# Cross attention and a max-out layer on one core: layer 1 of the first two batches from S W1 + S (-W2), and the softmax of later batches moved from layer 1 to layer 2

## The chip, the cores and the metric

The kernel runs on one core of one Trainium2 chip. The metric is the time of one execution on the device in microseconds (us), and lower is better. TensorE (PE) multiplies matrices, VectorE (DVE), ScalarE (ACT) and GpSimd (POOL) do elementwise work and reductions, and SyncE (SP) issues nearly all transfers. Each engine takes its instructions from a queue of its own, in the order in which the program names them; the order is written by hand here, and waits between engines follow from the data.

## The reference, cut to what matters

For each of 8 batches and 8 heads, 512 positions x and 32 states S, both 64 wide, read each other by attention. Both results of a batch are put together (512 + 32 rows of 8 x 64 = 512 columns) and go through a max-out layer with one pair of weights (512 x 1024) and an output weight (1024 x 512).

```python
def _attn_ref(x, state):                # x (8, 8, 512, 64), state (8, 8, 32, 64)
    scale = 1.0 / np.sqrt(D)
    a = softmax(scale * x @ state^T)      # 512 x 32 for each batch and head
    xread = a @ state
    a2 = softmax(scale * state @ x^T)     # 32 x 512
    sread = a2 @ x
    return concatenate([xread, sread], axis=2)

def _moe_ref(x, w1, w2, w_out):         # x: 8 * 544 rows of 512
    h1 = x @ w1
    h2 = x @ w2
    g = np.maximum(h1, h2)
    return g @ w_out
```

(The softmaxes are written out in the original, with the maximum subtracted.)

Two identities carry the kernel. First, max(h1, h2) = relu(h1 - h2) + h2, so out = relu(x (W1 - W2)) W_out + x (W2 W_out). Second, xread = a S, so that xread (W1 - W2) = a (S (W1 - W2)) with only 32 states a head: S W is made once for each batch, and layer 1 is A^T against it. The kernel keeps W1 - W2 and W2 W_out side by side in `wcat`, 1024 and 512 columns; "S W" is S times the first part (two pieces of 512 columns), "S Wc" times the second (the third piece).

## The kernel before

The parts that the change touches; cuts are marked with "...". `copy("A" | "V" | "P", ...)` is a copy on ACT, DVE or POOL. `bank()` takes the next of eight PSUM banks, which comes free when what it held eight takings earlier has been read out.

```python
    ...  # load_states(hb), cast_states(hb), states(hb): load, cast and transpose the states of half the batches into the block-diagonal sbd; after the change, of a slice of batches
    def compact_x(b, g):
        if g == 0:
            st[b]["xc"] = at.tile([128, H, NC * D], BF16, tag="xc", name="xc")
        copy("A", st[b]["xc"][:, 4 * g:4 * g + 4], xf_t[b][:, 4 * g:4 * g + 4])


    def d_xt(b):
        nc.sync.dma_start_transpose(out=st[b]["xt"], in_=st[b]["xc"].rearrange("p h w -> p (h w)"))
    ...
    def u_sc(b, g, mul=nc.gpsimd):
        u_exp(b, g)
        u_norm(b, g, mul)

    def u_exp(b, g):
        ...  # tiles
        p = bank()
        for i in range(4):
            for cp in range(2):
                k = 2 * i + cp
                nc.tensor.matmul(p[:, k * 64:k * 64 + 64],
                                 d["xt"][:, 4 * i + 2 * g + cp, :], sbd[:, b, 2 * i + g].rearrange("p u n -> p (u n)"),
                                 start=(k == 0), stop=(k == 7))
        nc.scalar.activation(out=d["e"][:, g].rearrange("p i c n -> p (i c n)"), in_=p, func=ACTF.Exp, scale=scale)

    def u_norm(b, g, mul):
        d = st[b]
        nc.vector.tensor_reduce(d["es"][:, g], d["e"][:, g].rearrange("p i c n -> p (i c) n"),
                                axis=mybir.AxisListType.X, op=ALU.add)
        nc.vector.reciprocal(d["er"][:, g], d["es"][:, g])
        mul.tensor_mul(
            d["a"][:, g].rearrange("p c i n -> p i c n"), d["e"][:, g],
            d["er"][:, g].rearrange("p (i c) -> p i c", i=4).unsqueeze(3).to_broadcast([128, 4, NC, Ns]))

    ...  # u_sr: the state's read, 32 small matmuls; u_at, u_xt: transposes on TensorE
    def d_at(b):
        AT[b] = keep.tile([128, 2, NC * 128], BF16, tag="at", name="aT")
        nc.sync.dma_start_transpose(out=AT[b].rearrange("p g (c t) -> p (g c) t", t=128),
                                    in_=st[b]["a"].rearrange("p g c i n -> p (g c i n)"))
    ...
    def u_sw(b, ch):
        pg = [bank(), bank()]
        for i in range(4):
            for g in range(2):
                nc.tensor.matmul(pg[g][32 * i:32 * i + 32, :], sbd[64 * g:64 * g + 64, b, 2 * i + g, g, :],
                                 wcat[64 * g:64 * g + 64, i, ch * 512:(ch + 1) * 512],
                                 start=True, stop=True)
        for g in range(2):
            copy("A" if g else "V", SW[b][:, g, ch * 512:(ch + 1) * 512], pg[g])
    ...  # u_sw01(q, engs): the same for batches 0 and 1 together, 256 columns: see the diff
    ...  # relu: on ACT or DVE, in turn where no engine is named
    def l1(b, fill, fs=range(NF), engs=None):
        if fs[0] == 0:
            R[b] = big.tile([128, NF, NC * 128], BF16, tag="r", name="r")
        for f in fs:
            p = bank()
            for g in range(2):
                nc.tensor.matmul(p, SW[b][:, g, f * 128:(f + 1) * 128], AT[b][:, g, :], start=(g == 0), stop=(g == 1))
            relu(R[b][:, f, :], p, engs and engs[f - fs[0]])
            run(*fill.get(f, ()))

    def l2(b, fill):
        r = R.pop(b)
        ob = big.tile([128, NC, DM], F32, tag="ob", name="ob")
        dst = out[b * L:b * L + S].rearrange("(p c) n -> p c n", c=NC)
        for c in range(NC):
            p = bank()
            cs = slice(c * 128, (c + 1) * 128)
            for g in range(2):
                nc.tensor.matmul(p, AT[b][:, g, cs], SW[b][:, g, FF:WC], start=(g == 0), stop=False)
            for f in range(NF):
                nc.tensor.matmul(p, r[:, f, cs], wo[:, f, :], start=False, stop=(f == NF - 1))
            copy("A" if c % 2 else "V", ob[:, c, :], p)
            if b == B - 1:
                nc.sync.dma_start(out=dst[:, c:c + 1], in_=ob[:, c:c + 1])
            run(*fill.get(NF + c, ()))
        if b < B - 1:
            nc.sync.dma_start(out=dst, in_=ob)
    ...
    def w_sub(q):
        cs = slice(q * 256, (q + 1) * 256)
        nc.vector.tensor_sub(wcat[:, :, cs], w1f[:, :, cs], w2f[:, :, cs])
    ...  # w_cast: W2 to bfloat16 on POOL; w_t: its transposes; w_wo: W2 W_out and its copy on ACT to wcat; ahead, fillers: see the diff
    for b in range(B):
        SW[b] = swt[:, b % 2]
    warm_up(9)
    cast_states(0)
    states(0)
    cast_x(0, (("V", slice(0, 4, 2)), ("A", slice(4, 8, 2)), ("V", slice(1, 4, 2)), ("P", slice(5, 8, 2))))
    u_xt(0, 0, "V")
    u_xt(0, 1, "A")
    u_sc(0, 0, nc.vector)
    u_sc(0, 1, nc.gpsimd)
    cast_x(1, (("P", slice(0, 4, 2)), ("P", slice(4, 8, 2)), ("A", slice(1, 4, 2)), ("A", slice(5, 8, 2))))
    w_cast(0)
    u_sr(0)
    u_xt(1, 0, "A")
    u_xt(1, 1, "V")
    u_at(0, "V")
    u_exp(1, 0)
    u_exp(1, 1)
    u_norm(1, 0, nc.gpsimd)
    u_norm(1, 1, nc.gpsimd)
    u_srt(0)
    nc.gpsimd.dma_start(out=wo, in_=moe_w_out.rearrange("(k p) n -> p k n", p=128))
    w_sub(0)
    w_sub(1)
    w_cast(1)
    u_sw01(0, "AA")
    u_at(1, "A")
    l1(0, {}, range(0, 2), "AA")
    l1(1, {}, range(0, 2), "VA")
    u_sw01(1, "VA")
    u_sr(1)
    w_t(0, 0, "V")
    l1(0, {}, range(2, 4), "AV")
    l1(1, {}, range(2, 4), "AA")
    w_sub(2)
    w_sub(3)
    u_srt(1)
    w_t(0, 1, "A")
    u_sw01(2, "AA")
    l1(0, {}, range(4, 6), "AA")
    l1(1, {}, range(4, 6), "VA")
    u_sw01(3, "VA")
    w_t(1, 0, "V")
    l1(0, {}, range(6, 8), "AV")
    l1(1, {}, range(6, 8), "AV")
    w_t(1, 1, "A")
    cast_x(2)
    compact_x(2, 0)
    compact_x(2, 1)
    d_xt(2)
    for i in range(4):
        w_wo(i)
    cast_states(1)
    u_sw(0, 2)
    u_sw(1, 2)
    ahead(3)
    l2(0, {8: [lambda: u_sc(2, 0), lambda: d_xt(3)], 9: [lambda: u_sc(2, 1)], 10: [lambda: u_sr(2)], 11: [lambda: d_at(2), lambda: u_srt(2)]})
    ahead(4)
    l2(1, {8: [lambda: u_sc(3, 0), lambda: d_xt(4), lambda: u_sw(2, 0)], 9: [lambda: u_sc(3, 1), lambda: u_sw(2, 1)],
           10: [lambda: u_sr(3), lambda: u_sw(2, 2)], 11: [lambda: d_at(3), lambda: states(1), lambda: u_srt(3)]})
    for b in range(2, B):
        fill = fillers(b)
        if b + LEAD + 1 < B:
            ahead(b + LEAD + 1)
        l1(b, fill)
        l2(b, fill)
        if b == B - 2:
            moe_sread()
```

A "slot" is a place in the loop: slots 0 to 7 follow the eight feature blocks of layer 1 (`l1`), slots 8 to 11 the four chunks of layer 2 (`l2`).

Of the kernel before, what the change touches and what calls it, by code (L numbers as in the profile page):

```python
# [15 lines left out]
def kernel(  # L16
# [46 lines left out]

    def run(*units):
        for u in units:
            u()
# [11 lines left out]
    def load_states(hb):  # L78
        nc.sync.dma_start(out=s_f[:, B * hb:B * hb + B],
                          in_=state[B // 2 * hb:B // 2 * hb + B // 2].rearrange("b (q h) n d -> (h n) (b q) d", q=2))  # L80

    load_states(0)
# [9 lines left out]
    load_states(1)  # L92
# [10 lines left out]
    w2b = stage.tile([128, 4, FF], BF16)  # L103
# [10 lines left out]
    def cast_states(hb):  # L114
        qs = slice(B * hb, B * hb + B)
        copy("V", s_bf[:, qs], s_f[:, qs].unsqueeze(2).to_broadcast([128, B, 2, D]))

    def states(hb):
        p = bank(BF16)
        for q in range(B):  # L120
            nc.tensor.transpose(p[:, q * 128:(q + 1) * 128], s_bf[:, B * hb + q].rearrange("p u d -> p (u d)"), ident)
        for g in range(2):
            copy("V", sbd[64 * g:64 * g + 64, B // 2 * hb:B // 2 * hb + B // 2, :, g, :],
                 p[64 * g:64 * g + 64].rearrange("p (b h n) -> p b h n", b=B // 2, h=H))
# [112 lines left out]
    def u_sw01(q, engs):  # L237
        pg = [bank(), bank()]
        for b in range(2):
            for i in range(4):  # L240
                for g in range(2):
                    nc.tensor.matmul(pg[g][32 * i:32 * i + 32, b * 256:(b + 1) * 256],  # L242
                                     sbd[64 * g:64 * g + 64, b, 2 * i + g, g, :],
                                     wcat[64 * g:64 * g + 64, i, q * 256:(q + 1) * 256],
                                     start=(b == 0), stop=(b == 1))
        for g in range(2):
            copy(engs[g], swt[:, :, g, q * 256:(q + 1) * 256], pg[g].rearrange("p (b w) -> p b w", b=2))
# [23 lines left out]
    def l2(b, fill):  # L271
# [3 lines left out]
        for c in range(NC):  # L275
            p = bank()
            cs = slice(c * 128, (c + 1) * 128)
            for g in range(2):
                nc.tensor.matmul(p, AT[b][:, g, cs], SW[b][:, g, FF:WC], start=(g == 0), stop=False)  # L279
            for f in range(NF):  # L280
                nc.tensor.matmul(p, r[:, f, cs], wo[:, f, :], start=False, stop=(f == NF - 1))  # L281
# [34 lines left out]
    def w_cast(ch):  # L316
        cs = slice(ch * 512, (ch + 1) * 512)
        for i in range(0, 4, 2):
            copy("P", w2b[:, i:i + 2, cs], w2f[:, i:i + 2, cs])

    def w_t(ch, half, eng):
        p = bank(BF16)
        for j in range(2):
            for k in range(4):
                f = 4 * ch + k
                nc.tensor.transpose(p[:, (4 * j + k) * 128:(4 * j + k + 1) * 128],
                                    w2b[:, 2 * half + j, f * 128:(f + 1) * 128], ident)
# [3 lines left out]
    def w_wo(i):  # L331
# [3 lines left out]
        copy("A", wcat[:, i, FF:WC], p)  # L335


    def ahead(n):
        if n < B:
            cast_x(n)  # L340
            compact_x(n, 0)
            compact_x(n, 1)
        if n + 1 < B:
            load_x(n + 1)

    def fillers(b):
        fill = {}
        n = b + LEAD
        if n < B:
            for slot, u in ((4, lambda: u_sc(n, 0)), (6, lambda: u_sc(n, 1)), (8, lambda: u_sr(n)),  # L350
                            (10, lambda: d_at(n)), (11, lambda: u_srt(n))):
                fill.setdefault(slot, []).append(u)
        if n + 1 < B:
            fill.setdefault(8, []).append(lambda: d_xt(n + 1))
        if b + 1 < B:
            for slot, ch in ((3, 0), (7, 1), (9, 2)):
                fill.setdefault(slot, []).append(lambda ch=ch: u_sw(b + 1, ch))
        return fill
# [3 lines left out]
    warm_up(9)  # L362
    cast_states(0)
    states(0)
    cast_x(0, (("V", slice(0, 4, 2)), ("A", slice(4, 8, 2)), ("V", slice(1, 4, 2)), ("P", slice(5, 8, 2))))
    u_xt(0, 0, "V")
    u_xt(0, 1, "A")
    u_sc(0, 0, nc.vector)
    u_sc(0, 1, nc.gpsimd)
    cast_x(1, (("P", slice(0, 4, 2)), ("P", slice(4, 8, 2)), ("A", slice(1, 4, 2)), ("A", slice(5, 8, 2))))  # L370
    w_cast(0)
    u_sr(0)
    u_xt(1, 0, "A")
# [84 lines left out]
```

## Time and profile before

| What | Value |
|---|---|
| Time, median of 3 runs | 171.58 us (169.97 to 173.24) |
| Span of the profiled run | 171.0 us |
| Busy: PE, DVE, ACT, POOL | 147.7, 80.3, 74.6, 36.8 us |
| Layer 2's matmuls r W_out (L281) | 253 recorded, 61.4 us busy, 379 ns each |
| Layer 1's matmuls (L267) | 120 recorded, 33.6 us busy, 409 ns each |
| Subtraction W1 - W2 on DVE (L314) | 4, 1797 ns each |
| Cast xc on ACT for the next batches (L58) | 12, 1054 ns each |
| Relus: ACT (L255), DVE (L257) | 35 of 608 ns, 29 of 673 ns |
| Product a on POOL (L182) | 15, 1113 ns each |
| Transposing transfers xt (6) and aT (6), issue to landing, median | 7.0 and 2.9 us |

How to read it: matmuls overlap, so that a row's busy time is longer than TensorE needs for them; where 8 stand in a row, the time from first to first is what one costs. PEld is the loading of weights into TensorE, beside its matmuls. The groups name lines of the kernel: L58, L60 and L62 are the copies on ACT, DVE and POOL for whatever tile; L154, L195, L213 and L230 are transposes of x, the state's read, the transposes of a and S W; L242 is S W of the first two batches, L172 the scores, L175 the exp, L179 and L181 the sum and its reciprocal, L279 and L281 layer 2, L295 the first layer for the states' rows, L326 the transposes of W2, L334 W2 W_out. Releasers are inferred: "PE <- DVE wcat" says that PE's wait ended when DVE had written wcat.

### The profile page before, as it was taken

To read this page: it belongs to the slowest core of one execution; us is meant where nothing else is said; L and a number is where in the kernel's file an instruction comes from. 1 tells how busy PE (TensorE), PEld (TensorE's weight loads), DVE (VectorE), ACT (ScalarE), POOL (GpSimd) and SP (SyncE) were. 2 spreads that over 40 slices of the span, in tenths; PEclk is the share of its full clock that TensorE was granted. 3 is DMA by queue.
4 is the path that set the end of the run, shared out by engine and by line. 5 is a ranking of instruction groups with operands and counts; after the bars stand their busy time and mean duration, and the time that the engine had idled before them with its cause. 6 is when DMAs were issued, how large, how long until landed. Compare 5 with 4: busy or idle time off the path is not lost.

```text
span 171.0 us, 3071 instructions
## 1 busy us (share of the span) xinstructions
PE 147.7 (86%) x1270; PEld 69.8 (41%) x1289; DVE 80.3 (47%) x139; ACT 74.6 (44%) x131; POOL 36.8 (22%) x44
## 2 busy tenths in 40 slices
PE   6554469499979999997998899799999999999991
PEld 2343434234425444443442344244434444744440
DVE  5561775926033446567345524832763643223410
ACT  3171355757665073690277119422802722305111
POOL 3108397400002604405302510400130000000000
PEclk9965558969999999999999999999999999999999
DMA  5999999800496289999459937620520500324033
GB/s 150 340 390 386 376 312 236 145 2 0 88 266 131 64 235 297 219 274 241 103 171 263 180 65 255 116 61 4 245 51 12 230 19 0 161 88 107 15 123 125
DMA packets 34366, 27.99 MB, mean 164 GB/s; under 512 B 21424, under 2 KB 30640, under 8 KB 33456
## 3 DMA queue, kind: packets, MB, share of 16 engines
q1 hardware_dynamic: 33312, 26.74, 55.1%
q0 software_dynamic: 1040, 1.05, 3.8%
q8 instruction: 10, 0.16, 0.4%
q14 instruction: 4, 0.03, 0.1%
HBM read 15.20 MB, written 8.91 MB: 141 GB/s over the span
## 4 chain that ended last, share of the span: by engine, by line
PE 69%; DVE 13%; ACT 11%; issue 3%; POOL 1%; DVEq 0%; ACTq 0%; POOLq 0%
PE ps L281 29%; PE ps L267 11%; PE ps L279 7%; DVE es L179 5%; PE ps L334 4%; ACT xc L58 3%; DVE r L257 3%; PE ps L230 2%; ACT r L255 2%; PE ps L109 2%; DVE wcat L314 2%; PE ps L295 2%; PE ps L305 2%; ACT e L175 2%; PE ps L154 2%
## 5 line engine op out<-in xcount | busy, mean ns | idle before, releaser
L281 PE MATMUL ps<-wo,r 128*128 128x512 bf16 x253 | 61.4, 379 | 3.7 <-DVE r L257 3.3
L281 PEld LDWEIGHTS <-r 128*128 128x128 bf16 x256 | 24.7, 98 | 35.9 <-DVE r L257 6.8
L267 PE MATMUL ps<-aT,swt 128*128 128x512 bf16 x120 | 33.6, 409 | 1.3 <-ACT swt L58 0.7
L58 ACT COPY ob<-ps 128x512 f32<-128x512 f32 x16 | 9.4, 585 | 57.0 <-PE ps L281 42.8
L182 POOL TENSOR_TENSOR a<-e,er 128x512 bf16<-128x512 bf16 x15 | 16.6, 1113 | 78.0 <-ACT e L175 37.4
L257 DVE TENSOR_SCALAR r<-ps 128x512 bf16<-128x512 f32 x29 | 19.4, 673 | 19.7 <-PE ps L267 19.4
L255 ACT ACTIVATE r<-ps 128x512 bf16<-128x512 f32 x35 | 20.8, 608 | 6.2 <-PE ps L267 4.7
L60 DVE CAST swt<-ps 128x512 bf16<-128x512 f32 x22 | 14.8, 678 | 17.4 <-PE ps L230 16.5
L60 DVE COPY ob<-ps 128x512 f32<-128x512 f32 x16 | 11.0, 688 | 20.2 <-PE ps L281 20.2
L279 PE MATMUL ps<-swt,aT 128*128 128x512 bf16 x57 | 17.7, 381 | 1.2 <-issue 0.6
L58 ACT CAST swt<-ps 128x512 bf16<-128x512 f32 x26 | 15.2, 598 | 7.7 <-PE ps L242 4.3
L267 PEld LDWEIGHTS <-swt 128*128 128x128 bf16 x128 | 11.6, 103 | 15.1 <-issue 3.9
L179 DVE TENSOR_REDUCE es<-e 128x16 f32<-128x512 bf16 x16 | 10.8, 678 | 11.3 <-ACT e L175 11.3
L62 POOL CAST xp<-xf 128x2048 bf16<-128x2048 f32 (+1 forms) x9 | 13.1, 1463 | 10.8 <-DMA xf<-in_x_dram 10.8
L58 ACT CAST xc<-xf 128x1024 bf16<-128x1024 f32 x12 | 12.0, 1054 | 0.0
L175 ACT ACTIVATE e<-ps 128x512 bf16<-128x512 f32 x16 | 9.8, 617 | 1.8 <-PE ps L172 1.8
L230 PE MATMUL ps<-wcat,sbd 64*32 64x512 bf16 x160 | 8.4, 386 | 0.5 <-ACT wcat L58 0.3
L172 PEld LDWEIGHTS <-xt 128*128 128x128 bf16 x128 | 6.2, 104 | 3.8 <-DVE xt L60 0.5
L154 PE MATMUL ps<-ident,xp 128*64 128x128 bf16 x64 | 3.1, 267 | 5.2 <-POOL xp L62 3.2
L172 PE MATMUL ps<-sbd,xt 128*128 128x64 bf16 x128 | 6.8, 202 | 0.9 <-ACT xt L58 0.4
L279 PEld LDWEIGHTS <-aT 128*128 128x128 bf16 x64 | 4.6, 97 | 6.7 <-issue 3.9
L334 PE MATMUL ps<-wo,w2t 128*128 128x512 bf16 x32 | 7.1, 379 | 0.0
(56 smaller groups left out, 101.8 us busy)
## 6 DMA issues: line engine op xcount, KB each, us to landing
xf<-in_x_dram SPq DMA_DIRECT2D x7, 1024.0 KB, 9.2
out_dram<-ob SPq DMA_DIRECT2D x7, 1024.0 KB, 4.4
w2f<-in_moe_w_dram SPq DMA_DIRECT2D x2, 1024.0 KB, 11.9
w1f<-in_moe_w_dram SPq DMA_DIRECT2D x2, 1024.0 KB, 13.4
xf<-in_x_dram SPq DMA_DIRECT2D x2, 512.0 KB, 4.6
wo<-in_moe_w_out_dram POOLq DMA_DIRECT2D x1, 1024.0 KB, 11.8
out_dram<-ob SPq DMA_DIRECT2D x4, 256.0 KB, 2.0
s_f<-in_state_dram SPq DMA_DIRECT2D x2, 256.0 KB, 9.7
```

What stands on the lines that cost most here:

```text
L58: nc.scalar.copy(o, i)
L60: nc.vector.tensor_copy(o, i)
L62: nc.gpsimd.tensor_copy(o, i)
L175: nc.scalar.activation(out=d["e"][:, g].rearrange("p i c n -> p (i c n)"), in_=p, func=ACTF.Exp, scale=scale)
L179: nc.vector.tensor_reduce(d["es"][:, g], d["e"][:, g].rearrange("p i c n -> p (i c) n"), axis=mybir.AxisListType.X, op=ALU.add)
L182: mul.tensor_mul(d["a"][:, g].rearrange("p c i n -> p i c n"), d["e"][:, g], d["er"][:, g].rearrange("p (i c) -> p i c", i=4).unsqueeze(3) ...
L255: nc.scalar.activation(out=o, in_=p, func=ACTF.Relu)
L257: nc.vector.tensor_scalar(o, p, scalar1=0.0, scalar2=None, op0=ALU.max)
L267: nc.tensor.matmul(p, SW[b][:, g, f * 128:(f + 1) * 128], AT[b][:, g, :], start=(g == 0), stop=(g == 1))
L279: nc.tensor.matmul(p, AT[b][:, g, cs], SW[b][:, g, FF:WC], start=(g == 0), stop=False)
L281: nc.tensor.matmul(p, r[:, f, cs], wo[:, f, :], start=False, stop=(f == NF - 1))
L334: nc.tensor.matmul(p, w2t[:, i, f, :], wo[:, f, :], start=(f == 0), stop=(f == NF - 1))
```

## The change

Two parts.

At the head, batches 0 and 1 need S (W1 - W2) before anything of layer 1 can start, and the subtraction of full-precision weights on DVE stands between the weights' landing and S W. The change multiplies S with W1 and with -W2 and lets PSUM add the two: twice the matmuls, and casts of W1 and negations of W2 to bfloat16 in place of the subtraction. The casts are spread over ACT, DVE and POOL. The negated copy also serves for the transposes behind W2 W_out, whose sign is turned back when the product is read out. The subtraction, which the later batches and the states' rows still need, moves behind layer 1 of batches 0 and 1. The states come in two loads with batches 0 and 1 alone in the first, and their block-diagonal copies are made in three steps (2, 3 and 3 batches). The warm-up has 5 matmuls in place of 9, and the order of the first softmaxes is different.

In the steady part, scores, exp, sums and products of batch b + 2, the casts xc of batch b + 3 and S W of batch b + 1 were spread over layer 1 and layer 2 of batch b. They are now all in the four slots of layer 2; layer 1 holds its matmuls and relus. The transposing transfer of xc moves from slot 8 to slot 11, behind that of a. In layer 2 of batch 0, the matmuls with W_out come ahead of those with S Wc.

The diff, cut:

```diff
...
+    def negate(eng, o, i):
+        if eng == "A":
+            nc.scalar.activation(out=o, in_=i, func=ACTF.Copy, scale=-1.0)
+        else:
+            (nc.vector if eng == "V" else nc.gpsimd).tensor_scalar(o, i, scalar1=-1.0, scalar2=None, op0=ALU.mult)
+
     def run(*units):
...
-    def load_states(hb):
-        nc.sync.dma_start(out=s_f[:, B * hb:B * hb + B],
-                          in_=state[B // 2 * hb:B // 2 * hb + B // 2].rearrange("b (q h) n d -> (h n) (b q) d", q=2))
-
-    load_states(0)
+    def load_states(bs):
+        nc.sync.dma_start(out=s_f[:, 2 * bs.start:2 * bs.stop],
+                          in_=state[bs].rearrange("b (q h) n d -> (h n) (b q) d", q=2))
+
+    first, rest = slice(0, 2), (slice(2, 5), slice(5, 8))
+    load_states(first)
     load_x(0, 2)
...
     load_x(2)
-    load_states(1)
+    load_states(slice(2, 8))
     load_x(3)
...
     wcat = consts.tile([128, 4, WC], BF16)
-    w2b = stage.tile([128, 4, FF], BF16)
+    w1b = stage.tile([128, 4, FF], BF16)
+    w2n = stage.tile([128, 4, FF], BF16)
     w2t = stage.tile([128, 4, NF, 128], BF16)
...
...
         for b in range(2):
-            for i in range(4):
-                for g in range(2):
-                    nc.tensor.matmul(pg[g][32 * i:32 * i + 32, b * 256:(b + 1) * 256],
-                                     sbd[64 * g:64 * g + 64, b, 2 * i + g, g, :],
-                                     wcat[64 * g:64 * g + 64, i, q * 256:(q + 1) * 256],
-                                     start=(b == 0), stop=(b == 1))
+            for k, w in enumerate((w1b, w2n)):
+                for i in range(4):
+                    for g in range(2):
+                        nc.tensor.matmul(pg[g][32 * i:32 * i + 32, b * 256:(b + 1) * 256],
+                                         sbd[64 * g:64 * g + 64, b, 2 * i + g, g, :],
+                                         w[64 * g:64 * g + 64, i, q * 256:(q + 1) * 256],
+                                         start=(b == 0 and k == 0), stop=(b == 1 and k == 1))
         for g in range(2):
...
             cs = slice(c * 128, (c + 1) * 128)
-            for g in range(2):
-                nc.tensor.matmul(p, AT[b][:, g, cs], SW[b][:, g, FF:WC], start=(g == 0), stop=False)
-            for f in range(NF):
-                nc.tensor.matmul(p, r[:, f, cs], wo[:, f, :], start=False, stop=(f == NF - 1))
+            mm = [(AT[b][:, g, cs], SW[b][:, g, FF:WC]) for g in range(2)]
+            rr = [(r[:, f, cs], wo[:, f, :]) for f in range(NF)]
+            mm = rr + mm if b == 0 else mm + rr
+            for k, (w, v) in enumerate(mm):
+                nc.tensor.matmul(p, w, v, start=(k == 0), stop=(k == NF + 1))
             copy("A" if c % 2 else "V", ob[:, c, :], p)
...
-    def w_cast(ch):
+    def w2_cast(ch, engs):
         cs = slice(ch * 512, (ch + 1) * 512)
-        for i in range(0, 4, 2):
-            copy("P", w2b[:, i:i + 2, cs], w2f[:, i:i + 2, cs])
+        for k in range(2):
+            negate(engs[k], w2n[:, 2 * k:2 * k + 2, cs], w2f[:, 2 * k:2 * k + 2, cs])
+
+    def w1_cast(ch):
+        cs = slice(ch * 512, (ch + 1) * 512)
+        copy("V", w1b[:, 0:2, cs], w1f[:, 0:2, cs])
+        copy("A", w1b[:, 2:4, cs], w1f[:, 2:4, cs])
...
                 nc.tensor.transpose(p[:, (4 * j + k) * 128:(4 * j + k + 1) * 128],
-                                    w2b[:, 2 * half + j, f * 128:(f + 1) * 128], ident)
+                                    w2n[:, 2 * half + j, f * 128:(f + 1) * 128], ident)
         copy(eng, w2t[:, 2 * half:2 * half + 2, 4 * ch:4 * ch + 4, :].rearrange("p j f t -> p j (f t)"),
...
             nc.tensor.matmul(p, w2t[:, i, f, :], wo[:, f, :], start=(f == 0), stop=(f == NF - 1))
-        copy("A", wcat[:, i, FF:WC], p)
-
-
-    def ahead(n):
-        if n < B:
-            cast_x(n)
-            compact_x(n, 0)
-            compact_x(n, 1)
-        if n + 1 < B:
-            load_x(n + 1)
+        negate("A", wcat[:, i, FF:WC], p)
+
         fill = {}
+
+        def put(slot, *units):
+            fill.setdefault(slot, []).extend(units)
+
         n = b + LEAD
         if n < B:
-            for slot, u in ((4, lambda: u_sc(n, 0)), (6, lambda: u_sc(n, 1)), (8, lambda: u_sr(n)),
-                            (10, lambda: d_at(n)), (11, lambda: u_srt(n))):
-                fill.setdefault(slot, []).append(u)
+            put(8, lambda: u_sc(n, 0))
+            put(9, lambda: u_sc(n, 1))
         if n + 1 < B:
-            fill.setdefault(8, []).append(lambda: d_xt(n + 1))
+            put(8, lambda: compact_x(n + 1, 0))
+            put(9, lambda: compact_x(n + 1, 1))
         if b + 1 < B:
-            for slot, ch in ((3, 0), (7, 1), (9, 2)):
-                fill.setdefault(slot, []).append(lambda ch=ch: u_sw(b + 1, ch))
+            for ch in range(3):
+                put(8 + ch, lambda ch=ch: u_sw(b + 1, ch))
+        if n < B:
+            put(10, lambda: u_sr(n))
+            put(11, lambda: d_at(n), lambda: u_srt(n))
+        if n + 1 < B:
+            put(11, lambda: d_xt(n + 1))
         return fill
         SW[b] = swt[:, b % 2]
-    warm_up(9)
-    cast_states(0)
-    states(0)
-    cast_x(0, (("V", slice(0, 4, 2)), ("A", slice(4, 8, 2)), ("V", slice(1, 4, 2)), ("P", slice(5, 8, 2))))
+    warm_up(5)
+    cast_states(first)
+    states(first)
+    cast_x(0, (("V", slice(0, 4, 2)), ("A", slice(4, 8, 2)), ("P", slice(5, 8, 2))))
     u_xt(0, 0, "V")
+    copy("V", st[0]["xp"][:, 1:4:2, :, 0:64], xf_t[0][:, 1:4:2].rearrange("p h (c d) -> p h c d", c=NC))
+    u_exp(0, 0)
     u_xt(0, 1, "A")
-    u_sc(0, 0, nc.vector)
-    u_sc(0, 1, nc.gpsimd)
+    u_norm(0, 0, nc.vector)
+    u_sc(0, 1, nc.vector)
     cast_x(1, (("P", slice(0, 4, 2)), ("P", slice(4, 8, 2)), ("A", slice(1, 4, 2)), ("A", slice(5, 8, 2))))
-    w_cast(0)
-    u_sr(0)
     u_xt(1, 0, "A")
+    u_at(0, "V")
     u_xt(1, 1, "V")
-    u_at(0, "V")
     u_exp(1, 0)
     u_exp(1, 1)
+    u_sr(0)
+    w2_cast(0, "AA")
     u_norm(1, 0, nc.gpsimd)
     u_norm(1, 1, nc.gpsimd)
+    nc.gpsimd.dma_start(out=wo, in_=moe_w_out.rearrange("(k p) n -> p k n", p=128))
+    w2_cast(1, "PP")
+    w1_cast(0)
     u_srt(0)
-    nc.gpsimd.dma_start(out=wo, in_=moe_w_out.rearrange("(k p) n -> p k n", p=128))
-    w_sub(0)
-    w_sub(1)
-    w_cast(1)
-    u_sw01(0, "AA")
+    u_sw01(0, "AV")
     u_at(1, "A")
-    l1(0, {}, range(0, 2), "AA")
+    u_sw01(1, "VA")
+    l1(0, {}, range(0, 2), "VA")
     l1(1, {}, range(0, 2), "VA")
-    u_sw01(1, "VA")
     u_sr(1)
+    l1(0, {}, range(2, 4), "VA")
+    l1(1, {}, range(2, 4), "VA")
+    u_srt(1)
     w_t(0, 0, "V")
-    l1(0, {}, range(2, 4), "AV")
-    l1(1, {}, range(2, 4), "AA")
-    w_sub(2)
-    w_sub(3)
-    u_srt(1)
     w_t(0, 1, "A")
-    u_sw01(2, "AA")
-    l1(0, {}, range(4, 6), "AA")
+    w1_cast(1)
+    u_sw01(2, "AV")
+    u_sw01(3, "VA")
+    l1(0, {}, range(4, 6), "VA")
     l1(1, {}, range(4, 6), "VA")
-    u_sw01(3, "VA")
     w_t(1, 0, "V")
-    l1(0, {}, range(6, 8), "AV")
-    l1(1, {}, range(6, 8), "AV")
+    l1(0, {}, range(6, 8), "VA")
+    l1(1, {}, range(6, 8), "VA")
     w_t(1, 1, "A")
     d_xt(2)
+    for bs in rest:
+        cast_states(bs)
+    for q in range(4):
+        w_sub(q)
     for i in range(4):
         w_wo(i)
-    cast_states(1)
+    for bs in rest:
+        states(bs)
     u_sw(0, 2)
     u_sw(1, 2)
-    ahead(3)
-    l2(0, {8: [lambda: u_sc(2, 0), lambda: d_xt(3)], 9: [lambda: u_sc(2, 1)], 10: [lambda: u_sr(2)], 11: [lambda: d_at(2), lambda: u_srt(2)]})
-    ahead(4)
-    l2(1, {8: [lambda: u_sc(3, 0), lambda: d_xt(4), lambda: u_sw(2, 0)], 9: [lambda: u_sc(3, 1), lambda: u_sw(2, 1)],
-           10: [lambda: u_sr(3), lambda: u_sw(2, 2)], 11: [lambda: d_at(3), lambda: states(1), lambda: u_srt(3)]})
+    cast_x(3)
+    load_x(4)
+    l2(0, {8: [lambda: u_sc(2, 0), lambda: compact_x(3, 0), lambda: compact_x(3, 1), lambda: d_xt(3)],
+           9: [lambda: u_sc(2, 1)], 10: [lambda: u_sr(2)], 11: [lambda: d_at(2), lambda: u_srt(2)]})
+    cast_x(4)
+    load_x(5)
+    l2(1, {8: [lambda: u_sc(3, 0), lambda: u_sw(2, 0), lambda: compact_x(4, 0)],
+           9: [lambda: u_sc(3, 1), lambda: u_sw(2, 1), lambda: compact_x(4, 1)],
+           10: [lambda: u_sr(3), lambda: u_sw(2, 2)], 11: [lambda: d_at(3), lambda: u_srt(3), lambda: d_xt(4)]})
     for b in range(2, B):
         if b + LEAD + 1 < B:
-            ahead(b + LEAD + 1)
+            cast_x(b + LEAD + 1)
+            if b + LEAD + 2 < B:
+                load_x(b + LEAD + 2)
         l1(b, fill)
         if b == B - 2:
```

More of the change, by code (lines that the diff above doesn't have):

```diff
@@ L112, with cast_states, states @@
     s_bf = stage.tile([128, 2 * B, 2, D], BF16)
[L114 to L118, printed above, removed]
+    def cast_states(bs):
+        qs = slice(2 * bs.start, 2 * bs.stop)
+        copy("V", s_bf[:, qs], s_f[:, qs].unsqueeze(2).to_broadcast([128, qs.stop - qs.start, 2, D]))
+    def states(bs):
         p = bank(BF16)
-        for q in range(B):
-            nc.tensor.transpose(p[:, q * 128:(q + 1) * 128], s_bf[:, B * hb + q].rearrange("p u d -> p (u d)"), ident)
+        n = bs.stop - bs.start
+        for q in range(2 * n):
+            nc.tensor.transpose(p[:, q * 128:(q + 1) * 128], s_bf[:, 2 * bs.start + q].rearrange("p u d -> p (u d)"), ident)
         for g in range(2):
-            copy("V", sbd[64 * g:64 * g + 64, B // 2 * hb:B // 2 * hb + B // 2, :, g, :],
-                 p[64 * g:64 * g + 64].rearrange("p (b h n) -> p b h n", b=B // 2, h=H))
+            copy("V", sbd[64 * g:64 * g + 64, bs, :, g, :],
+                 p[64 * g:64 * g + 64, 0:256 * n].rearrange("p (b h n) -> p b h n", b=n, h=H))
     sread_t = consts.tile([128, 4, B * Ns], BF16)
```

## The prediction

> **What bounds the kernel now.** I read the page's slices first, then the chain of work that ended last, in order of time, then busy times in windows, and last the timelines of ScalarE (ACT) and of the transposing transfers. The slices (forty, 4.275 us each): TensorE's busy tenths and its granted clock.
>
> ```profile
> PE   6554469499979999997998899799999999999991
> PEclk9965558969999999999999999999999999999999
> ```
>
> Two kernels in one. Up to 41 us TensorE is half idle and often at half clock; from 41 us it is nearly always busy at full clock, and what remains to be won hides behind "busy". The windows show where: stretch, length, then busy us (instructions) of PE, PEld, DVE, ACT, POOL, the granted clock, DMA share, GB/s.
>
> ```profile
> 10.00:27.00 17.00, 9.46 (x127) 6.33 (x129) 9.48 (x16) 7.73 (x14) 10.71 (x13) 0.50 1.08 362
> 27.00:34.00 7.00, 4.52 (x91) 2.42 (x90) 6.33 (x8) 4.56 (x9) 3.49 (x3) 0.98 0.99 167
> 34.00:37.00 3.00, 3.00 (x8) 0.89 (x8) 0.25 (x1) 1.54 (x3) 0.00 (x0) 0.51 0.02 4
> ...
> 95.00:102.30 7.30, 7.14 (x71) 3.29 (x72) 2.52 (x6) 1.07 (x2) 2.30 (x3) 1.00 0.71 101
> 102.30:111.00 8.70, 7.41 (x63) 2.94 (x66) 5.27 (x10) 6.54 (x12) 1.86 (x2) 1.00 0.65 183
> ```
>
> The last two are one batch: most of layer 2 of batch 3, then layer 1 of batch 4 with the start of its layer 2. ACT has 1.07 us of work in the first and 6.54 in the second, DVE 2.52 and 5.27. The chain in the second:
>
> ```profile
> 103.21 1.89 ACT xc L58 x2
> 105.10 0.27 ACT r L255
> 105.48 0.61 ACT r L255
> 106.08 0.47 ACT swt L58
> 106.56 0.50 ACT r L255
> 107.06 0.50 ACT e L175
> 107.58 0.70 DVE es L179
> 108.37 0.25 DVE er L181
> 108.62 0.55 DVE r L257
> 109.17 0.60 DVE es L179
> 109.96 0.64 DVE r L257
> 110.64 0.39 PE ps L281
> ```
>
> Not one TensorE piece between 103.21 and 110.64: the two xc casts, the exps and the sums of the next batches stand in front of the relus in ACT's and DVE's queues, and layer 2 cannot start without the last relu. At the head the two subtractions W1 - W2 hold S W back (waits: waiter, releaser, us in all, times, longest):
>
> ```profile
> PEld L242 <- DVE wcat L314: 5.5, 2, 3.6
> PE ps L242 <- DVE wcat L314: 5.2, 2, 3.4
> ```
>
> **What the Trainium skill says.** "TensorE: Matmul & The Clock Gate", Back-to-back issue gap: N/2.4 + 2.5 ns, 216 ns for 512 columns. The chain has 1.73 us for eight L281 matmuls, 216 ns each; I count TensorE's work with that and not with the 379 ns of the page's rows, which overlap. Same page, Part 1: The HAM clock gate: half rate until some 3.4 us of sustained activity, and again after an idle window. The trace agrees: 0.50 through 10 to 27 us, and 0.51 in 34 to 37, after the wait for the second subtractions; eight L267 there took 3.65 us instead of 1.73. Same page, Architectural detail: ScalarE and VectorE take their queues strictly in order. The chain shows it: relus behind the casts that nothing yet needs.
>
> **Part 1: layer 1 of batches 2 to 6.** First L267 of batches 2 to 6 and first L295 after them, in TensorE's timeline: 70.74, 86.31, 102.31, 118.32, 133.00, 146.42; so 15.57, 16.00, 16.01, 14.68, 13.42 us a batch. A full batch's work: L267 16 x 0.216 = 3.46; layer 2 40 x 0.216 = 8.64; S W 3 x 0.34; scores 2 x 0.23; state read 0.37; its transpose 0.06. Sum 14.0. Batch 6 has no softmax, 13.12 by count, and took 13.42; I allow the same 0.3: 14.3. The change takes all but the relus (0.5 us spacing on ACT, 0.6 on DVE) out of layer 1. A pair of relus (max 0.69) is shorter than the 0.86 us in which TensorE makes their two tiles, so layer 1 becomes TensorE's. Gain 1.27 + 1.70 + 1.71 + 0.38 = 5.1 us, batch 6 nothing.
>
> Layer 2 must carry it. ACT there: two ob 0.585, two exp 0.617, three swt 0.598, two xc 1.054, sread 0.27: 7.2 us at most by rows, some 6.6 back to back. DVE: two ob 0.69, three swt 0.68, two sums 0.68, small ones 1.0: 5.8. TensorE in the same stretch: 14.0 - 3.46 = 10.5. Following the slots: ob of chunk 1 leaves its bank 0.6 us after its last matmul, and no bank is asked for again within eight allocations before it is free. ACT's line at that point is exp 0.62, xc 1.05 and swt 0.6 from the end of the scores, 2.3 us, and chunk 1 and its S W take TensorE 2.5. No new bound.
>
> **Part 2: from W2 W_out to layer 1 of batch 2.** Before: L334 starts at 40.91, so 29.83 us to 70.74. After: 32 x 0.216 = 6.9; twelve state transposes at 0.056 (eight took 0.45 at 70.24), 0.67, which fill the wait for the last wcat; S Wc for two batches 0.68; layer 2 of batch 0 9.6 as before (49.81 to 59.43), now without its 0.55 us wait for swt, as r W_out goes first; layer 2 of batch 1 11.3 (59.43 to 70.74) less 0.45 for the transposes taken out. The four subtractions move under W2 W_out: 4 x 1.21 (their shortest) after 1.0 of casts, done 6 us after its start, before the states come. Sum 28.8 with 0.1 for swt. Gain 1.0.
>
> **Part 3: the head.** Walked engine by engine, at half clock from 10.6 us as before. States come with half the bytes: S cast at 3.3, copies to 5.0, so the first xp casts start when x lands (5.0) and its transposes at 5.75 instead of 8.13. Then the in-order chain: exp 8.15, second a on DVE done at 13.2 (before on POOL 14.6), transposes of batch 1 at 10.75 and 14.2 (2.05 each), exps 16.8 and 17.65 (before 18.73), state read, sums until 20.85. ACT negates W2 (two casts of 1.05, as xc) and casts half of W1 until 21.1; DVE casts the other half (0.69, as s_bf) until 21.5. S W starts at 21.55, before 22.66. It is 32 matmuls instead of 16 a quarter, +0.56 us at half clock (the first sixteen ended 0.56 later), +0.34 warm, four times: about +1.8. Layer 1 f 0 to 3 ends at 29.9, before 30.35. Then ACT has a relu, sread, w2t (1.0) and its half of W1 (1.05) in line: 32.9, DVE 31.7. The wait shrinks from 1.73 us but does not vanish. S W of both quarters to 34.3, swt beside it, then 16 L267 and 16 transposes: 38.7 at full clock, 40.4 if the gap at 31 to 33 turns the clock down as it does now. Before 40.91. POOL's two negations have no row in the profile; as its casts of that size (1.04) they end near 25, and even at twice that well before 31. Gain 0.5 to 2.2; more if the earlier start keeps the clock up in 11 to 17, where two blocks of transposes take 2.05 instead of 1.1 us. I take 2.0.
>
> **Sum.** 5.1 + 1.0 + 2.0 = 8.1; 171.6 - 8.1 = 163.5, rounded to 163.3 as Part 1's 0.3 is partly bank waits that may go as well.
>
> **Rivals.** (a) A late transpose. The xt transfer moves from slot 8 to slot 11 behind that of aT, and the next scores read it in slot 8 of the next batch. From the start of layer 2: chunk 0 2.16, scores and S W 0.57, chunk 1 2.16, second scores 0.23, so 5.1; ACT's exp behind the ob copy to 6.1; sum and reciprocal to 7.1; POOL's product 1.05 to 8.2; the issue of aT 1.24: xt goes out at 9.5 and is read at 10.5 + 3.46 + 2.16 = 16.2. Clean ones landed in 4.3 to 4.8 us (44.0, 52.1, 105.1), those issued 2 us after an output store and a load of x in 9.3 to 10.0 (62.2, 73.1, 89.1). Now they go 12 us after those two, which land in 9.7 at most: clean, 2 us of margin. If contended, 2.6 us for each of four batches: 174. (b) Layer 2 bound by evictions: 1 us a batch would leave 168; 6.6 of 10.5 us speaks against. (c) The head gives nothing, as doubled S W and the cast line eat the earlier start: 165.5. (d) The clock stays up in the head: 160 to 161.
>
> **Range and chances.** Part 1 is counted from matmuls and nearly sure (4 to 6); Part 2 0 to 1.5; the head -0.5 to 4.5. 159.5 to 167. The runs of before spread over 3.3 us, which the range includes. 2% faster is 168.15: it needs (a) or two misses to fail. Faster 0.92, within 2% 0.07, slower 0.01.
>
> **What would show it.** L267 to L267 of batches 2 to 5 near 14.3 each; no ACT or DVE pieces but a last relu in their layer 1 in the chain; xt landing under 5 us; L334 starting at 38 to 40; L242 waiting for w1b, not wcat. Wrong if scores wait for a DMA, if L281 in layer 2 waits for banks, or if L334 starts after 41.

## The result, and the profile after

The changed kernel takes 163.97 us (median of four runs, 163.43 to 164.48) against 171.24 (four runs, 169.97 to 173.24): ratio 0.960, 95% interval 0.953 to 0.967. A second comparison gave 164.17 us and 0.966 (0.959 to 0.973). The prediction was 163.3 us, 159.5 to 167.0. (The ratios leave out executions in which the chip was in a slower state, so that a ratio is not the quotient of the two medians.)

The slices of the changed kernel's page, TensorE busy and granted clock (4.04 us each):

```profile
PE   6267389499999999999999999999999999999990
PEclk9999999999999999999999999999999999999998
```

From 32 us to the last matmuls TensorE has no slice below 9. The head is still thin. The clock row reads full everywhere, which it was not, as is shown below.

One batch from first layer-1 matmul to first layer-1 matmul, in windows (length, then busy us of PE, PEld, DVE, ACT, POOL, clock, DMA share, GB/s). First batch 3 of the kernel before, then batches 3 and 4 of the changed one:

```profile
86.31:102.31 16.00, 14.55 (x129) 6.23 (x130) 7.79 (x15) 7.62 (x14) 4.16 (x4) 1.00 0.81 181
```

```profile
80.16:94.48 14.32, 14.32 (x132) 6.68 (x131) 8.08 (x15) 8.15 (x14) 3.98 (x4) 1.00 0.72 203
94.48:108.79 14.31, 14.31 (x132) 6.67 (x130) 8.08 (x15) 8.15 (x14) 2.09 (x2) 1.00 0.45 129
```

The engines do the same work in both, give or take half a microsecond; only its place differs. TensorE's 14.3 us now fill the batch without a gap. The chain of the changed kernel in batch 4, where before there were 7.4 us without a TensorE piece:

```profile
94.64 3.45 PE ps L277 x16
98.09 2.16 PE ps L292 x10
100.25 0.23 PE ps L181 x8
100.48 0.34 PE ps L239 x8
100.83 2.26 PE ps L292 x10
```

L277 is layer 1, L292 layer 2, L181 the scores, L239 S W of the later batches, L163 the transposes of x. Layer 1 takes 3.45 us, its sixteen matmuls at 0.216. In the waits of the head, S W (L252) now waits for the cast of W1 in place of the subtraction, and little less:

```profile
PEld L252 <- DVE w1b L60: 4.8, 2, 2.5
PE ps L252 <- DVE w1b L60: 4.4, 2, 2.3
```

### The profile page after: what moved, and what is told of

Read it like the earlier page. It is cut to its first block, busy times and chain, and to the rows that moved or that the text cites. A ratio compares the mean times of both kernels' runs of the same rounds, so it can differ in the third digit from the quotient of the medians.

```text
span 161.7 us, 3207 instructions
## 1 busy us (share of the span) xinstructions
PE 145.4 (90%) x1349; PEld 72.0 (45%) x1349; DVE 87.0 (54%) x150; ACT 77.9 (48%) x130; POOL 37.1 (23%) x41
## 4 chain that ended last, share of the span: by engine, by line
PE 85%; DVE 7%; DMA 3%; ACT 2%; issue 1%; SPq 0%
PE ps L292 43%; PE ps L277 17%; PE ps L350 4%; PE ps L239 4%; PE ps L181 3%; DMA xf<-in_x_dram 3%; PE ps L306 2%; PE ps L316 2%; PE ps L204 2%; PE ps L163 2%; PE ps L252 2%; DVE w1b L60 2%; DVE sbd L60 1%; DVE es L188 1%; PE ps L314 1%; PE ps L222 1%
## 5 line engine op out<-in xcount | busy, mean ns | idle before, releaser
L292 PE MATMUL ps<-wo,r 128*128 128x512 bf16 x256 | 60.5, 379 | 0.0
L292 PEld LDWEIGHTS <-r 128*128 128x128 bf16 x256 | 24.8, 98 | 29.7 <-issue 0.4
L267 DVE TENSOR_SCALAR r<-ps 128x512 bf16<-128x512 f32 x32 | 22.1, 691 | 17.3 <-PE ps L277 17.2
L191 POOL TENSOR_TENSOR a<-e,er 128x512 bf16<-128x512 bf16 x14 | 15.1, 1080 | 70.7 <-DVE er L190 35.6
L277 PE MATMUL ps<-aT,swt 128*128 128x512 bf16 x128 | 29.4, 380 | 0.3 <-ACT swt L58 0.3
L265 ACT ACTIVATE r<-ps 128x512 bf16<-128x512 f32 x32 | 19.2, 600 | 7.4 <-PE ps L277 7.0
L58 ACT CAST swt<-ps 128x512 bf16<-128x512 f32 x24 | 13.9, 588 | 11.8 <-PE ps L239 9.7
L292 PE MATMUL ps<-swt,aT 128*128 128x512 bf16 x64 | 19.1, 382 | 0.3 <-DVE swt L60 0.3
L277 PEld LDWEIGHTS <-swt 128*128 128x128 bf16 x128 | 12.1, 98 | 14.6 <-issue 0.6
L60 DVE CAST swt<-ps 128x512 bf16<-128x512 f32 x24 | 15.7, 661 | 4.9 <-PE ps L252 3.2
L181 PE MATMUL ps<-sbd,xt 128*128 128x64 bf16 x128 | 7.2, 205 | 2.2 <-ACT xt L58 1.1
L181 PEld LDWEIGHTS <-xt 128*128 128x128 bf16 x128 | 6.2, 105 | 5.8 <-DVE xt L60 1.4
L239 PE MATMUL ps<-wcat,sbd 64*32 64x512 bf16 x160 | 8.1, 386 | 0.0
L292 PEld LDWEIGHTS <-aT 128*128 128x128 bf16 x64 | 4.7, 97 | 7.0 <-issue 3.8
L252 PE MATMUL ps<-w1b,sbd 64*32 64x256 bf16 x64 | 2.6, 338 | 4.4 <-DVE w1b L60 4.4
```

The costliest lines, as they stand in the source:

```text
L58: nc.scalar.copy(o, i)
L60: nc.vector.tensor_copy(o, i)
L181: nc.tensor.matmul(p[:, k * 64:k * 64 + 64], d["xt"][:, 4 * i + 2 * g + cp, :], sbd[:, b, 2 * i + g].rearrange("p u n -> p (u n)"), start= ...
L191: mul.tensor_mul(d["a"][:, g].rearrange("p c i n -> p i c n"), d["e"][:, g], d["er"][:, g].rearrange("p (i c) -> p i c", i=4).unsqueeze(3) ...
L265: nc.scalar.activation(out=o, in_=p, func=ACTF.Relu)
L267: nc.vector.tensor_scalar(o, p, scalar1=0.0, scalar2=None, op0=ALU.max)
```

## The experiments

The theory: ScalarE's and VectorE's in-order lines held layer 1 of the later batches (5 us), and the new head brings some 2 us more. Eleven runs test it.

**The kernel before, once more**

> The kernel before once more, for a second profile of its head. If the half-rate clock of the head is a matter of where the run falls, W2 W_out starts anywhere from 38 to 41 us; if it follows from the program's own gaps, at 40.9 again, with 0.50 granted from about 10 to 27 us and again near 34 to 37 us. Either way layer 1 of batches 3 and 4 takes the same 16.0 us a batch.

172.06 us in one run. W2 W_out starts at 40.12 us (40.91 in the first profile), the recorded clock is 0.50 again through 10 to 18 and in 34 to 36 us, and batches 3 and 4 take 16.01 us each. The head moves, the batches do not. Three further profiles with the same head (in the experiments below) have W2 W_out at 40.58, 40.60 and 37.87. So one pair of profiles says little of the head.

**The steady part alone** (head of before; the loop of after, with the second half's state transposes left in slot 11)

```diff
-    def ahead(n): ...           # xc casts ahead of layer 1
-            for slot, u in ((4, lambda: u_sc(n, 0)), (6, lambda: u_sc(n, 1)), (8, lambda: u_sr(n)), ...
+            put(8, lambda: u_sc(n, 0))       # fillers and the calls of l2(0), l2(1) as after
```

> The head of before, layer 1 and 2 of after. My theory (the in-order lines of ScalarE and VectorE in front of the relus held TensorE in layer 1): 14.3 us for each of batches 2 to 5, 5.1 us off the time, so 166 us, ratio 0.970. Rival (most of the gain is the head's, and the steady part's gain shows only with it): ratio 0.985 to 1.0.

167.46 us, ratio 0.975 (0.966 to 0.985). Batches 2 to 5 take 14.31 or 14.32 us each. That fits the theory: the gain of layer 1 needs nothing of the new head. By the ratio it is 4.2 us, with the 5.1 expected inside the interval (2.6 to 5.8).

**The head alone** (after's program up to layer 2, the loop of before)

```diff
-    cast_x(3)
-    load_x(4)
-    l2(0, {8: [lambda: u_sc(2, 0), lambda: compact_x(3, 0), ...
+    ahead(3)                                  # fillers, ahead and the loop as before
+    l2(0, {8: [lambda: u_sc(2, 0), lambda: d_xt(3)], ...
```

> The head of after with the states' copies ahead of layer 2, layer 1 and 2 of before. My theory: the two parts add up, so what is left of the measured 7.3 us after 5.1: some 2.2 us, 169 us, ratio 0.987; by the two profiles alone (W2 W_out at 36.6 for 40.9) it would be 4.3 us, 0.975. Batches 2 to 5 at 15.6, 16.0, 16.0, 14.7 us as before. Rival (head is hidden anyway): ratio 1.0.

169.21 us, ratio 0.987 (0.979 to 0.996); W2 W_out at 37.59; batches 16.01, 16.01, 16.01 and 14.67 us. The two parts add up: 0.975 and 0.987 make 0.963, the whole was 0.960 and 0.966.

**The xc casts alone moved**

```diff
             cast_x(n)
-            compact_x(n, 0)
-            compact_x(n, 1)
+            if n < 5:
+                compact_x(n, 0)
+                compact_x(n, 1)
...
-            fill.setdefault(8, []).append(lambda: d_xt(n + 1))
+            fill.setdefault(8, []).append(lambda: compact_x(n + 1, 0))
+            fill.setdefault(8, []).append(lambda: compact_x(n + 1, 1))
+            fill.setdefault(9, []).append(lambda: d_xt(n + 1))
```

> Before, with only the two xc casts of each later batch moved from ahead of layer 1 to slot 8 of layer 2, and their transfer to slot 9. If the casts alone held layer 1 (2.0 us at the front of ScalarE's line), a batch takes 14.3 to 14.6 us in place of 16.0. If it is the whole line, VectorE is next: four relus 2.4, two sums 1.4, two reciprocals 0.4, two swt 1.2, 5.4 us in front of a TensorE that needs 4.6, so 15.0 to 15.3 us a batch.

169.02 us in one run. Batches 2 to 5 take 14.68, 14.73, 14.68 and 14.67 us: between the two expectations, so neither holds as written.

**The softmax alone moved**

```diff
-            for slot, u in ((4, lambda: u_sc(n, 0)), (6, lambda: u_sc(n, 1)), (8, lambda: u_sr(n)),
-                            (10, lambda: d_at(n)), (11, lambda: u_srt(n))):
+            for slot, u in ((8, lambda: u_sc(n, 0)), (9, lambda: u_sc(n, 1)), (10, lambda: u_sr(n)),
+                            (11, lambda: d_at(n)), (11, lambda: u_srt(n))):
```

> Before, with only scores, exp, sum and product moved to slots 8 and 9, the state's read to 10 and aT to 11; xc casts and S W stay in layer 1. If the casts were the cause, a batch stays at 15.5 to 16.0 us. If the whole line counts, ScalarE has 2.75 us ahead of its first relu and 5.8 us in all against TensorE's 4.1; the eight banks hide a part: 14.8 to 15.3 us a batch.

165.20 us in one run. Batches 2 to 5 take 14.42 or 14.43 us, below both expectations, though the casts still stand ahead of the relus. ScalarE's timeline in batch 4 of this run:

```profile
97.33 2.00 ACT L58 CAST xc<-xf 128x1024 bf16<-128x1024 f32 x2
99.22 1.09 ACT L255 ACTIVATE r<-ps 128x512 bf16<-128x512 f32 x2
```

Layer 1 began at 96.54, its first relus on ScalarE came 2.7 us later, and TensorE did not stop: VectorE's relus and the free banks carried it. So moving one thing saves 1.3 us a full batch, moving the other 1.6, and both 1.7. Neither is the cause alone; the loss was in their sum. What both expectations overlooked is a second reserve: layer 2's first chunk needs the last relu only after its own 0.43 us and seven matmuls of 0.216, so 1.95 us into layer 2. The lines may run some 6.5 us (4.6 of TensorE's work and these 1.95) before TensorE waits. The profiles agree with this count. In batch 4 of before the last relu ended at 110.6, 8.3 us after the start of layer 1 at 102.31: 1.8 beyond the 6.5, and the batch lost 1.7 us against the 14.3 of after. In the casts-only run it ended 6.9 us after the start at 99.84, 0.4 beyond, and the batch lost 0.4:

```profile
106.15 0.63 DVE L257 TENSOR_SCALAR r<-ps 128x512 bf16<-128x512 f32 x1
```

In the softmax-only run the last relu ended 5.2 us after the start, inside the reserve, and TensorE did not wait. S W, which the change moves too, costs little where it was: in this run two of its three pieces are still in layer 1, at 0.1 us a batch over the 14.31.

A comparison of this kind lies in the profile of before: batch 5 has no xc cast any more and took 14.68 us where batches 3 and 4 took 16.0. The casts-only run gives the same 14.7 to all four.

**The transfer of xc behind the store and the load**

```diff
-            put(11, lambda: d_xt(n + 1))
...
                 load_x(b + LEAD + 2)
+        if 2 < b and b + LEAD < B:
+            d_xt(b + LEAD)
         l1(b, fill)
```

> After, with the xt transfer of batches 5 to 7 behind the output store and the next load of x instead of ahead of them. If an xt transfer behind those two lands in 9 to 10 us as in the profile of before, the scores of batch 5 wait some 5 us and those of 6 and 7, behind a store alone, below 1 us each: 5 to 7 us more than after. If the transfers do not hold one another up here, 0 to 1 us more.

177.29 us, 13.3 more than after. TensorE's timeline in batch 3:

```profile
93.11 0.61 PE L181 MATMUL ps<-sbd,xt 128*128 128x64 bf16 x8 [5.18 <-DMA xt<-xc]
93.65 0.63 PE L239 MATMUL ps<-wcat,sbd 64*32 64x512 bf16 x8
94.21 1.04 PE L292 MATMUL ps<-swt,aT 128*128 128x512 bf16 x2
95.03 3.01 PE L292 MATMUL ps<-wo,r 128*128 128x512 bf16 x8
```

Behind the store and the load the transfer landed in 9.3 us and the scores waited 5.18, as expected. Two terms were too small. Behind a store alone it took 6.4 and 6.5 us, and the scores waited 1.92 and 1.88, where below 1 was written. And the gap cost the clock: the eight L292 took 3.0 us in place of 1.9 by the same row, the window 93 to 96 us shows 0.50, and the batch is 7.3 us longer with a wait of 5.2. The next two batches are 2.1 us longer each. The rest of the 13.3 is the head: W2 W_out at 38.60 in this run, 36.61 in after. In after itself the transfers land in 4.4 to 4.5 us and the scores come 2.2 us later (issued at 79.19, landed at 83.6, scores at 85.77).

**The subtraction back in the new head**

```diff
-            for k, w in enumerate((w1b, w2n)):
+            for k, w in enumerate((wcat,)):
...
-    w1_cast(0)
+    w_sub(0)
+    w_sub(1)
...
-    w1_cast(1)
+    w_sub(2)
+    w_sub(3)
```

> After, with the subtraction W1 - W2 back in place of the two products: two subtractions where the first casts of W1 stood, two where the second stood, all the rest of the new head kept. Theory A (the double product is what shortens the head): S W of the first quarter waits for the subtractions to 22.7 us as before and W2 W_out starts 2 to 4 us later than 36.6; 166 to 168 us. Theory B (the new order gives the gain, and the product's extra matmuls eat what the missing subtraction saves): W2 W_out within 1 us of 36.6, time within 1 us of after's 164.0.

166.22 us, ratio 0.972 (0.965 to 0.978), W2 W_out at 39.64. The end of theory A holds: without the double product the change loses some 2 us of its 7 (1 to 2 by the ratios, 2.05 and 2.25 by the medians). What is left of the head's gain is small, 0.972 beside the 0.975 of the steady part alone. TensorE's waits in its timeline:

```profile
21.39 0.63 PE L252 MATMUL ps<-wcat,sbd 64*32 64x256 bf16 x16 [2.87 <-DVE wcat L325]
23.39 0.63 PE L252 MATMUL ps<-wcat,sbd 64*32 64x256 bf16 x16 [0.40 <-DVE wcat L325]
...
32.09 0.41 PE L252 MATMUL ps<-wcat,sbd 64*32 64x256 bf16 x16 [1.47 <-DVE wcat L325]
33.22 0.41 PE L252 MATMUL ps<-wcat,sbd 64*32 64x256 bf16 x16 [0.72 <-DVE wcat L325]
```

The first step of theory A does not hold: the first S W starts at 21.39, not at 22.7, and little later than with the product (20.14 to 20.76). But each quarter needs a subtraction of its own, and they follow one another on VectorE. Of the 3.0 us by which W2 W_out is later in this profile, the clock has a part: layer 1's eight matmuls from 33.83 on and the transposes behind them took 3.6 us, in after 2.2 (from 32.25).

**More warm-up**

```diff
     states(first)
+    warm_up(6)
     cast_x(0, ...
```

> After, with six more warm-up matmuls behind the state transposes, in the 2.2 us in which TensorE waits for x. In the profile of after, sixteen transposes of x take 1.0 us in 6 to 16 us, which is the rate of half clock, though the granted clock reads 1.00. If the rate is half indeed[...], the transposes take 0.55 us and S W starts 1 to 2 us earlier: 162.5 to 163.5 us. If they are bound otherwise, no change from 164.0.

165.04 us, ratio 0.969 (0.957 to 0.982): no gain. The rate did rise. The second block of transposes in after and in this run, at a recorded 1.00 in both:

```profile
8.75 1.07 PE L163 MATMUL ps<-ident,xp 128*64 128x128 bf16 x16
```

```profile
8.79 0.64 PE L163 MATMUL ps<-ident,xp 128*64 128x128 bf16 x16
```

It fell again by 13.90, where a block takes 1.06 at a recorded 0.50. S W started at 20.17, no earlier than the 20.15 of after's second profile. Yet the way from the first transposes to S W was shorter: 13.5 us here (6.67 to 20.17), 14.4 in the first profile of after and in four others with this head, 14.2 in after's second, which has one block at 0.64. The warm-up took back a part: TensorE stood in its matmuls until 6.67, though VectorE's first cast of x was done at 6.18. And behind the later wait for w1b the clock fell: eight matmuls of layer 1 took 3.09 us from 32.30 on, in after 1.90 from 32.25 on, and W2 W_out started at 37.85. So the transposes' rate counts in the head, and what it is worth without these two losses stays open.

**After once more, and two attempts to do better**

> The changed kernel once more, for a second profile of its head and as the measure for the two beside it: 163.5 to 164.5 us. If the start of W2 W_out moves with the clock as it did in the runs with the same head (36.6 here, 37.6 and 38.6 in two others), it falls anywhere from 36.6 to 38.6; batches 2 to 5 take 14.3 us each whatever the head does.

164.17 us (163.42 to 165.08), W2 W_out at 36.59, batches 2 to 5 14.31 or 14.32 us each.

```diff
     l1(1, {}, range(0, 2), "VA")
+    w1_cast(1)
     u_sr(1)
...
-    w1_cast(1)
```

> After, with the second casts of W1 moved up behind layer 1's first two features, so that they no longer stand behind the relus and the w2t copies. If the 2.1 us wait for w1b at 28.9 us is what remains of the head, S W of the third quarter starts near 29.0, the clock does not fall after it, and the time drops by 2 us or a little more, to 161.5 to 162 us. If the negated W2 from POOL (done at 28.2) or a landing takes its place, by below 1 us.

163.15 us (162.61 to 163.41), ratio 0.958 (0.953 to 0.963): 1.0 us less, not 2. The wait for w1b is gone and S W of the third quarter follows the transposes at 30.18. Yet in this run layer 1 before it ran at half clock until 26.7 us. The same eight matmuls in three profiles, of after, of after again and of this one:

```profile
23.70 2.01 PE L277 MATMUL ps<-aT,swt 128*128 128x512 bf16 x8
```

```profile
23.09 2.65 PE L277 MATMUL ps<-aT,swt 128*128 128x512 bf16 x8
```

```profile
23.40 3.34 PE L277 MATMUL ps<-aT,swt 128*128 128x512 bf16 x8
```

So W2 W_out starts at 36.20. Whether the edit itself shifts the clock is not settled by one profile; the first two of these are one and the same program and differ by 0.6 us.

```diff
-    w2_cast(1, "PP")
     w1_cast(0)
+    w2_cast(1, "PV")
...
         w_wo(i)
-    for bs in rest:
-        states(bs)
+        if i > 1:
+            states(rest[i - 2])
```

> As the one before, with one of POOL's two negations (5.54 us for both) moved to VectorE behind the first cast of W1, and the state transposes of batches 2 to 4 put between the third and fourth product W2 W_out instead of behind the fourth, so that their copies are done before swt. If the wait for swt in layer 2 of batch 0 (0.46 us) is those copies, it goes: 160.8 to 161.8 us, 0.3 to 0.6 less than the one before. If DVE's longer line at 21 us delays swt of batches 0 and 1, 162 or more.

162.07 us (six runs, 161.76 to 162.6), ratio 0.952 (0.948 to 0.956), beside 0.966 for after in the same comparison: this version beats both kernels. Layer 2 of batch 0 no longer waits for swt; its first chunk:

```profile
44.64 1.90 PE L292 MATMUL ps<-wo,r 128*128 128x512 bf16 x8
46.38 0.59 PE L292 MATMUL ps<-swt,aT 128*128 128x512 bf16 x2
```

From first to next 1.74 us, eight times 0.216; in after it was 2.19 (44.90 to 47.09). Most of that is paid elsewhere: six of the transposes now stand ahead of the fourth product, where all twelve filled the wait for its copy, and layer 2 starts 8.63 us after W2 W_out instead of 8.29. From W2 W_out to layer 1 of batch 2 it is 29.13 us here, 29.25 in the version before and 29.24 in after. The run changed two things at once beyond the one before, so the 1.1 us between them are not split; the two profiled spans differ by 0.4.

## Why the prediction was right

**Part 1** held to the digit: 14.3 us a batch predicted, 14.31 measured; the four batches took 62.26 us before and 57.25 after, 5.0 saved where 5.1 was written. Its mechanism was right but told too simply. "Stand in front of the relus" suggests that each of them costs; the runs show a threshold, with casts and softmax each costing little (0.1 and 0.4 us a batch) once the other is gone.

**Layer 2 carries it**, as counted: TensorE waits for no bank and no eviction in it. Rival (b) is out. **Rival (a)**, the late transfer, did not happen because of where it stands in the queue; the run with it two places later shows that the danger was real, and the 2 us of margin were 2.2. The prediction's line for ScalarE in layer 2, 7.2 us "by rows", adds up to 6.6 by its own terms; nothing rests on it.

**Part 2**: 28.8 us predicted, 29.24 measured (36.61 to 65.85). The step that failed is "with 0.1 for swt": the four copies of the states began at 44.05, took 2.26 us with their spacing of 0.56, and swt came at 47.04, which cost 0.46. The better version moves them and has no such wait, but gains 0.1 us by it in all.

**Part 3**, the head, was sized about right, in part by luck. W2 W_out with the old head started at 40.91, 40.12, 40.58, 40.60 and 37.87 (mean 40.0), with the new one, product and all, at 36.61, 36.59, 37.59 and 38.60 (mean 37.3): 2.7 us for the 2.0 taken, and the head's own ratio of 0.987 makes 2.2. The walk put that start at 38.7 to 40.4, and all four came earlier. Three of its steps failed.

S W started at 20.14 to 20.76, not 21.55. The largest slip is a line misread. "2.05 each" for the transposes of batch 1 is this row of before, and its 32 are two blocks:

```profile
15.25 2.05 PE L154 MATMUL ps<-ident,xp 128*64 128x128 bf16 x32 [3.22 <-POOL xp L62]
```

In after the two blocks took 1.14 and 1.06 us, and one of them stands on the chain to S W. (The 3.65 us for eight L267 is a row too, and is to be set against 1.90, not 1.73.)

"At half clock from 10.6 us as before": blocks of sixteen transposes took 1.06 us from 6.36 us on in the first profile of after and from 8.14 on in the second, up to some 24 us.

"The wait shrinks from 1.73 us": it was 2.06 us in the first profile of after, 1.75 in two pieces in the second, and only stood 2 us earlier. The clock's fall after that wait, which I had as a branch, happens in some runs and not in others, with either head. Rival (c) is out; rival (d), the clock staying up in the head, is not what the rates show.

Behind that wait is POOL. Its negations, assumed at 1.04 us each and "even at twice that" harmless, took 2.77:

```profile
22.68 5.54 POOL L68 TENSOR_SCALAR w2n<-w2f 128x1024 bf16<-128x1024 f32 x2
```

They ended at 28.2, before they were needed. But they pushed POOL's cast of x to 28.2, and VectorE's second w1b, assumed at 0.69, stood beside it:

```profile
28.22 1.91 POOL L62 CAST xp<-xf 128x2048 bf16<-128x2048 f32 x1
29.06 1.80 DVE L60 CAST w1b<-w1f 128x1024 bf16<-128x1024 f32 x1
```

The two together in the better version:

```profile
25.39 1.89 POOL L62 CAST xp<-xf 128x2048 bf16<-128x2048 f32 x1
26.92 1.09 DVE L60 CAST w1b<-w1f 128x1024 bf16<-128x1024 f32 x1
```

In both, w1b ended 0.73 us after POOL had. The second w1b did so, to 0.01 us, in all six profiles in which it began while POOL was at work (it took 1.09 to 1.89 us), and in the run with the late transfer, where it began after POOL's cast, it took 0.68. So this cast did not run slowly beside POOL; it waited for POOL's instruction to end. The old head shows the like: the second pair of subtractions took 3.53 us in before, with POOL's cast from 29.77 to 31.66, and 2.35 in the softmax-only run, where that cast began at 31.97.

The sum: 5.0 + 0.6 + 2.7 is 8.3; measured were 7.3 by the medians. (The spans of the two first profiles differ by 9.3, as the one of before has the latest start of W2 W_out of five.) Some 0.55 us were given back at the very end: from the last layer-2 row to the end of the span takes 5.55 to 5.6 us in the five profiles with the old head and 6.1 in after. It is 6.1 also with the old loop behind the new head and with the subtraction put back, and 6.5 in the run with the late transfer. What differs there stays open. The rest is within the spread of single runs. That 163.3 came so near 164.0 is luck in part: the head gave somewhat more than was written, Part 2 and the end less.

## What to carry to other kernels

Where a TensorE stage waits for the last of its evictions, add up what stands in each in-order line from the stage's start to that eviction, and compare it with TensorE's work plus the reserve of banks and of the next stage's first matmuls; work moved out pays until the sum fits, and no further. Look in the profile for a repetition that already lacks the suspected work: it is a free experiment. Work given to an idle engine is not free where another engine waits for that one: POOL's negations did not delay what reads them, but, through POOL's next cast, one on VectorE. And a transfer that the next stage reads belongs in its queue ahead of bulk loads and stores, with the margin worked out from a contended landing as well as from a clean one.

## What the runs showed of the hardware

The recorded clock can read 1.00 where the rate is half. The Trainium skill ("TensorE: Matmul & The Clock Gate", Seeing it yourself) warns that the clock's trace events have been unreliable; the runs agree. In the first profile of after, blocks of sixteen transposes took 1.06 us at a recorded 1.00; in the second, of the same program, the block at 8.14 took as long at a recorded 0.50, and in the run with more warm-up the one at 8.79 took 0.64 at 1.00. At the start even the warm-up matmuls read 1.00, though nine took 4.02 us in before and five 2.31 in after, so that each of the four more costs 0.43 us, twice the 0.216 of equal matmuls in layer 2. The spacing of equal matmuls is the safer measure.

The moment at which the clock comes up differs between runs of one program: eight matmuls of layer 1 took 2.01 and 2.65 us in two profiles of after. Between programs with the same head the start of W2 W_out differs by up to 3 us (37.87 to 40.91 with the old one), which is more than most edits of the head bring; of these 3 us, 1.5 are the clock (eight matmuls of layer 1 in 3.65 or 2.17 us) and 1.2 the subtractions beside POOL.

A cast on VectorE, 128 x 1024 from float32 to bfloat16 (the second w1b), took 0.68 us when POOL had ended its cast before, and up to 1.89 when it began while POOL was at work; it ended 0.72 or 0.73 us after POOL's instruction in these six profiles.

Multiplying by -1 on POOL while converting 128 x 1024 elements took 2.77 us, converting the same shape alone 1.04.

A transposing transfer of xc landed in 4.3 to 4.5 us where it was issued ahead of the output store, in 6.4 or 6.5 directly behind a 1 MB store and in 9.3 behind a store and a load.
